# Nystrom attention and two gated MLPs on one core: landmark sums of the second batch by matrix products, softmax exponentials group by group, another order

## Chip, cores and metric

One core of a Trainium2 chip runs the kernel. The metric is the device time of one execution in microseconds (us), median over runs. The profile is of one further execution.

## What is computed

Everything is float32 in and out. The reference, cut to what matters:

```python
def _attn_ref(q, k, v):                       # q, k, v: 4 batches, 8 heads, 576 tokens, 64 wide
    q_lm = q.reshape(B, H, 32, 18, D).mean(axis=3)      # 32 landmarks, each the mean of 18 tokens
    k_lm = k.reshape(B, H, 32, 18, D).mean(axis=3)
    A, Bm, C = sm(q, k_lm), sm(q_lm, k_lm), sm(q_lm, k)   # scaled row softmax, with maximum and sum
    Z = Bm.transpose(0, 1, 3, 2) / (norm1(Bm) * norminf(Bm) + 1e-06)
    for _ in range(6):
        Z = 2 * Z - Z @ Bm @ Z
    return A @ Z @ C @ v
x = attn.transpose(0, 2, 1, 3).reshape(2304, 512)
x = ((x @ w_a) * (x @ w_b)) @ w_out             # 512 -> 1536 -> 512
h = x @ w_in; x = (h * tanh(softplus(h))) @ w_out2      # 512 -> 2048 -> 512
```

## The kernel before

The attention of batch b is a set of steps (function attention, from L132). kl and ql (lm_sum) sum groups of 18 tokens of k and q, which lie with (head, width) on the 128 partitions and the tokens along the row. sB and BB make the small softmax Bm, NS is one of six Newton steps for Z, sC0 and sC1 are the two halves of the scores of landmarks against all keys, whose maxima go to tile stC and whose exponentials to tile E; ET, U and M finish to a 128x128 matrix MT. A0 and A1 (function A) make the two halves of the scores of all queries against the landmarks, transpose them into tile sa (128 partitions x 576, that is 18 groups of 32 columns), subtract the maximum of each group and take the exponential; A0n and A1n (function An) divide by the sums of the groups, transpose back and store a high and a low part (tile at), since the matrix products of the MLPs run as three products of split float32 numbers.

MT is folded into the weights w_a and w_b (fold, named f0, f1, F0, F1 in the order, matrix products ps_bm<-wab,mt, result tile bm). The slots s0 to s11 are products of at and bm (ps_ab<-at,bm, 6 at a time) whose two halves are multiplied (tg, g); o0 to o7 are products with w_out (ps_o<-g,wo). Weights arrive as 64-bit words and are turned to float32 by the units c0 to c19 (to_f32, L366 to L384: one ScalarE and four VectorE instructions each; tiles stg, wab, f, wo). c0 to c3 make the first half of w_a and w_b that f0 needs, c4 to c7 the second, c8 to c11 the first w_out blocks.

Batches 0 and 1, the first twelve slots and c0 to c19 are recorded in the order of a written list (ORDER_1; + marks a step of batch 1, a digit a few filler products that nothing reads). VectorE, ScalarE and TensorE keep that order, so an instruction that waits holds all that stands behind it on its engine. GpSimd work and transfers are placed by the scheduler; every transfer is issued on SyncE's queue and they share 16 DMA engines. Behind ORDER_1 come the slots 12 to 95 with the steps of batches 2 and 3 between them (STEADY), then the second MLP, which the change does not touch.

By the subtraction for the fourth of the next w_out blocks, a little behind the end of ORDER_1 (wo<-f,wo, 136.79 us in the profile), both programs have done the same VectorE work apart from what the change adds and takes out; soon behind it their VectorE rows are the same, one by one.

Of the kernel before, what the change touches and what calls it, by code (L numbers as in the profile page):

```python
# [8 lines left out]
F32 = mybir.dt.float32  # L9
# [8 lines left out]
LM = 32  # L18
# [10 lines left out]


@with_exitstack
def nystrom_moe_kernel(ctx: ExitStack, tc: tile.TileContext, q, k, v, w_a, w_b, w_out1, w_in2, w_out2, out):
    nc = tc.nc
    NT = B * S
    gp = nc.gpsimd
# [41 lines left out]
    def bank(tag):  # L77
        return two.get(tag, ps).tile([128, 512], F32, tag=tag, bufs=2, name=f"ps_{tag}")
# [53 lines left out]
    def attention(ap, b, kt, qt, vt0=None):  # L132

        x = {}
        first = b == 0
# [2 lines left out]
        def sm(shape, nm, bufs=1, tag=None):  # L138
            return ap.tile(shape, F32, tag=tag or nm, bufs=bufs, name=nm)
# [3 lines left out]

        def lm_sum(src, nm):
            x[nm] = sm([128, 4, LM], nm)
            for j in range(0, 4, 2):
                if first and nm == "ql":
                    p = bank("o1")
                    for _ in range(3):
                        pe.matmul(p[:, 0:128], ident, x["kl"].rearrange("p j l -> p (j l)"), start=True, stop=True)  # L150
                held(ve.tensor_reduce(
                    out=x[nm][:, j:j + 2], in_=src[:, j:j + 2].rearrange("p j (t k) -> p j t k", k=BLK), axis=AX, op=ALU.add,
                ))
                yield
# [132 lines left out]
        def A(r):  # L287
            p = pair("A%d" % r)
            tile4(p, lambda o, rows, j: (o[:, 0:288], x["kl"][rows, j, :], qt[rows, j, 288 * r:288 * r + 288]))
            if r == 0:  # L290
                x["sa"] = sm([128, 2, 2, 288], "sa", tag="E")
            sa = x["sa"][:, r]
            yield
            for c in range(2):
                ve.transpose(out=sa[:, c], in_=p[:, c, 0:288])
            sa3 = sa.rearrange("p c (n l) -> p (c n) l", l=LM)
            ss = x["ss", r] = sm([128, 18, 4], "stA", 2)
            yield
# [41 lines left out]

    N_UNITS, N_SLOTS = 20, 12
    ORDER_1 = """
        kl kl ql ql c0 sB sC0 sB c0 sB sC1 4 c1 sB sC0 BB 2 c2 sC1 BB c3 sC1 NS 2 c1 sC1 c2 c3 sC1 c0 c1 NS
        ET0 NS c2 c3 NS 2 ET0 c0 ET1 NS NS c4 c1 A0 ET1 c2 NS 1 c5 A0 U NS c6 NS A0 NS c7 c3 NS A0 NS U NS c0
        NS NS c1 NS NS c2 M A0n M A1 c3 A0n f0 A0n f0 +kl A0n f0 A0n +kl | s0 +ql s0 s0 s1 +ql s1 A1 A1 +sC0
        +sC1 +sC0 A1 +sC1 A1n A1n A1n +sC1 A1n s0 c4 +sC1 A1n s1 c5 c6 +sC1 +sB s1 +sB s0 +ET0 c7 s1 s0 c4 +sB
        s2 +ET0 +sB s1 s2 +ET1 c5 c6 +BB +ET1 c7 c4 s2 c8 +BB +U s2 c5 s2 +NS +U s2 s3 +NS +NS c6 +NS s3 c7 s3
        +NS +NS c4 +NS c5 +NS +NS c6 +NS c7 +NS +NS f1 s3 c8 s3 c8 s3 +NS c8 f1 c8 +NS c9 +NS f1 +NS c8 +NS s4
        c9 +M c9 s4 s4 c9 +M c9 s5 s4 c9 +A0 c8 s5 c9 s4 s5 c10 s4 +A0 s6 s5 F0 c10 s6 c10 s5 +A0 c11 s5 s6 F0
        s7 s6 +A0 c11 +A1 c11 s7 s6 c11 s7 c12 s6 c11 +A0n c11 c11 +A0n +A0n F0 +A0n +A0n s7 F1 c10 s7 c10 s7  # L350
        F1 s8 c12 c12 c10 F1 s8 s8 c10 s9 s8 c12 o0 s9 s8 c12 s8 +A1 c13 s9 +A1 o0 s10 o1 s9 s10 c13 +A1 c13
        s9 c13 c14 s10 s9 c13 o1 s11 s10 c14 s10 o2 c14 s11 s10 c14 c15 c14 s11 o2 c15 c15 o3 +A1n c15 c16
        +A1n o4 o3 c16 c16 o5 c15 o4 c17 +A1n c17 +A1n o6 c17 o5 c16 +A1n c16 o7 o6 s11 c17 s11 s11 c17 c18 o7
        c18 c18 c18 c18 c19 c19 c19 c19 c19
    """

    def stage(src, shape, early):
# [626 lines left out]
```

## Time and profile before

| what | value |
|---|---|
| median of 3 runs | 856.5 us (854.84 to 857.36) |
| the profiled execution | 852.74 us, of which 850.7 us are the span of its instructions |
| TensorE busy | 794.7 us (93%), 5802 matrix instructions |
| VectorE busy | 565.8 us (67%) |
| ScalarE busy | 342.1 us (40%) |
| GpSimd busy | 153.2 us (18%) |
| DMA | 180.85 MB, mean 213 GB/s |

Times in the profile are microseconds from the span's start. A float32 product shows as two TensorE records. L56 is the line of the helper that records every ScalarE, VectorE and TensorE instruction; tiles tell them apart.

### The profile page before, as it was taken

Reading aid. Unit: us, or ns where it says so; the run is one execution under the profiler, and the core shown is the slowest. Engines: PE = TensorE matmul, PEld = TensorE weight load, DVE = VectorE, ACT = ScalarE, POOL = GpSimd, SP = SyncE. Lnnn points to the kernel's source line nnn. Section 1 sums busy time; section 2 is a strip of 40 time slices with the busy share of each in tenths; the row PEclk is TensorE's granted clock in tenths of the full one; section 3 lists DMA queues with packets and bytes.
Section 4 is the critical chain, followed back from the end, with each engine's and each line's share of the span. In section 5 each row is a group of like instructions: output and inputs, shape, how many; then the busy total and the mean of one; then the engine's idle time right before and its main releaser. Section 6 shows DMA issues by size and latency. Waiting matters only on the chain.

```text
span 850.7 us, 14559 instructions
## 1 busy us (share of the span) xinstructions
PE 794.7 (93%) x5802; PEld 691.9 (81%) x5802; DVE 565.8 (67%) x1027; ACT 342.1 (40%) x684; POOL 153.2 (18%) x144
## 2 busy tenths in 40 slices
PE   5666999999999999999988999999999999999997
PEld 4444887987887888787987898988988989988986
DVE  7899977895575488888985678768433347433433
ACT  3335454444323445444443444345332334332332
POOL 0011222222230232122234335320000000000000
PEclk9798899999999999999999899999999999999999
DMA  9736467458227338777376857788655445654501
GB/s 357 306 120 229 160 214 246 179 206 319 81 85 255 163 113 314 247 265 238 115 251 274 302 215 259 264 310 336 247 196 212 173 171 200 227 213 179 186 1 74
DMA packets 47891, 180.85 MB, mean 213 GB/s; under 512 B 4176, under 2 KB 12368, under 8 KB 38480
## 3 DMA queue, kind: packets, MB, share of 16 engines
q1 hardware_dynamic: 47824, 179.93, 58.9%
q8 instruction: 45, 0.74, 0.3%
q14 instruction: 22, 0.18, 0.1%
HBM read 126.44 MB, written 53.48 MB: 211 GB/s over the span
## 4 chain that ended last, share of the span: by engine, by line
PE 75%; DVE 14%; DMA 6%; issue 3%; ACT 2%; SPq 0%; POOL 0%; ACTq 0%; DVEq 0%
PE ps_ab L56 33%; PE ps_o L56 21%; PE ps_bm L56 11%; PE ps_at L56 10%; DVE f L56 5%; DMA kt<-in_k_dram 3%; DMA wi2d<-f 2%; DVE tg L56 1%; DVE f L378 1%; DVE bm L56 1%; DMA wo2d<-f 1%; DVE kl L56 1%; ACT f L374 1%; DVE x2acc L56 1%; DVE s L56 1%
## 5 line engine op out<-in xcount | busy, mean ns | idle before, releaser
L56 PE MATMUL ps_ab<-xc,wc 128*128 128x384 f32 x1008 | 201.7, 340 | 4.8 <-DVE u2s L56 3.1
L56 PE MATMUL ps_ab<-at,bm 128*128 128x288 f32 x1152 | 192.0, 307 | 13.4 <-DVE tg L56 6.9
L56 PEld LDWEIGHTS ps_ab<-at,bm 128*128 128x128 f32 x1152 | 165.4, 194 | 41.9 <-issue 11.8
L56 PEld LDWEIGHTS ps_ab<-xc,wc 128*128 128x128 f32 x1008 | 181.8, 189 | 16.9 <-DVE u2s L56 3.4
L56 PE MATMUL ps_o<-g,wo 128*128 128x288 f32 x1152 | 180.0, 298 | 3.1 <-DVE x2acc L56 2.1
L56 PEld LDWEIGHTS ps_o<-g,wo 128*128 128x128 f32 x1152 | 161.0, 188 | 15.4 <-issue 5.9
L519 POOL TENSOR_TENSOR g<-tg,g 128x288 fp32r<-128x288 f32 x96 | 87.1, 908 | 268.0 <-ACT g L56 268.0
L56 ACT ACTIVATE m<-c 128x384 f32<-128x384 f32 x96 | 50.2, 523 | 189.6 <-DVE c L56 189.5
L56 PE MATMUL ps_bm<-wo,g 128*128 128x512 f32 x288 | 95.5, 396 | 0.3 <-ACT g L56 0.3
L56 PE MATMUL ps_at<-wo,g 128*128 128x512 f32 x288 | 82.9, 395 | 0.0
L56 DVE TENSOR_TENSOR g<-m,g 128x384 fp32r<-128x384 f32 x96 | 66.7, 696 | 23.0 <-ACT g L56 23.0
L56 PE MATMUL ps_o<-wo,g 128*128 128x512 f32 x288 | 79.6, 393 | 0.0
L56 ACT ACTIVATE g<-tg 128x288 fp32r<-128x288 f32 x96 | 42.4, 442 | 79.9 <-DVE tg L56 79.7
L56 DVE SCALAR_TENSOR_TENSOR f<-stg,f 128x512 uint32<-128x512 uint32 x88 | 72.1, 823 | 1.6
L56 PEld LDWEIGHTS ps_at<-wo,g 128*128 128x128 f32 x288 | 54.3, 189 | 10.7
L56 DVE TENSOR_TENSOR tg<-ps_ab,ta 128x288 f32<-128x288 f32 x96 | 43.2, 451 | 29.7 <-PE ps_ab L56 21.9
L56 ACT ACTIVATE ta<-ps_ab 128x288 f32<-128x288 f32 x96 | 38.9, 405 | 57.4 <-PE ps_ab L56 56.9
L56 PEld LDWEIGHTS ps_o<-wo,g 128*128 128x128 f32 x288 | 53.6, 188 | 9.1
L56 PEld LDWEIGHTS ps_bm<-wo,g 128*128 128x128 f32 x288 | 53.7, 189 | 7.0 <-ACT g L56 0.6
L56 ACT ACTIVATE g<-m 128x384 fp32r<-128x384 f32 x96 | 50.3, 523 | 2.6
L56 DVE TENSOR_TENSOR c<-ps_ab,m 128x384 f32<-128x384 f32 x24 | 13.4, 557 | 50.6 <-PE ps_ab L56 50.6
L56 PE MATMUL ps_bm<-wab,mt 64*32 64x512 f32 x384 | 39.3, 644 | 6.2 <-DVE bm L56 6.2
(138 smaller groups left out, 755.1 us busy)
## 6 DMA issues: line engine op xcount, KB each, us to landing
wc<-wcd SPq DMA_DIRECT2D x16, 1792.0 KB, 7.3
wo<-wod SPq DMA_DIRECT2D x16, 1024.0 KB, 4.9
stg<-in_moe_w_out_dram SPq DMA_DIRECT2D x28, 512.0 KB, 4.5
wcd<-wc SPq DMA_DIRECT2D x8, 1792.0 KB, 7.1
wab<-wabd SPq DMA_DIRECT2D x10, 1024.0 KB, 6.3
stg<-in_moe_w_in_dram SPq DMA_DIRECT2D x16, 512.0 KB, 5.1
wod<-wo SPq DMA_DIRECT2D x8, 1024.0 KB, 6.7
stg<-in_moe_w_a_dram SPq DMA_DIRECT2D x12, 512.0 KB, 6.4
```

The lines of the kernel that those rows point to most:

```text
L56: i = f(*a, **kw)
L374: i = ac.engine.activation(dst, hi.bitcast(F32), AF.Abs)
L378: i = ve.engine.tensor_scalar(dst, dst, F32_TINY, F32_HUGE, op0=ALU.max, op1=ALU.min)
L519: gp.tensor_tensor(t[:, 1], tg, t[:, 0].bitcast(F32), op=ALU.subtract)
```

## The change

For batch 1 the landmark sums are no longer VectorE reductions over kt and qt. The host hands in two more inputs (q1, k1: tokens on 126 partitions, 7 groups of 18; five blocks of 512 columns), six transfers bring them in ahead of the second four weight blocks, and for each of 4 column blocks five products with a 126 x 7 matrix of ones (blk) write the sums to a PSUM bank; one ScalarE copy per tensor takes them out. In A, for batches 0 and 1, the subtraction and the single exponential over 576 columns are replaced by a small product (minus the scaled maximum) and 18 exponentials of 32 columns with the maximum as bias and the sum of the group as second output; An loses its sum. The low part of at goes to VectorE for all four halves of batches 0 and 1 (before: for the first alone, the others on GpSimd). ORDER_1 is another list; N_UNITS and N_SLOTS are the same.

```diff
+    blk = const.tile([128, 7], F32, name="blk")
+        ve.tensor_reduce(out=blk, in_=ident[:, 0:126].rearrange("p (l k) -> p l k", k=BLK), axis=AX, op=ALU.add)
+    def load_tokens():
+        out = []
+        for src in (k1, q1):
+            ts = []
+            for i in range(0, 5, 2):
+                if src is q1 and i:
+                    t = main.tile([128, 2, 2, S // 2], F32R, tag="AT", bufs=6, name="tok").bitcast(F32).rearrange("p a b s -> p (a b s)")
+                else:
+                    t = main.tile([128, 4, 288], F32, tag="x2", bufs=4, name="tok").rearrange("p a s -> p (a s)")
+                w = min(2, 5 - i)
+                nc.sync.dma_start(out=t[0:126, 0:DM * w], in_=src[:, DM * i:DM * (i + w)])
+                ts.append(t)
+            out.append(ts)
+        return out
...
         def lm_sum(src, nm):
             x[nm] = sm([128, 4, LM], nm)
+            if tokens:
+                p, ts = bank("o1"), tokens[nm == "ql"]
+                for j in range(4):
+                    for i in range(5):
+                        n, r = (4, 72) if i == 4 else (7, 126)
+                        f0 = DM * (i % 2) + 128 * j
+                        pe.matmul(p[:, LM * j + 7 * i:LM * j + 7 * i + n], ts[i // 2][0:r, f0:f0 + 128], blk[0:r, 0:n], start=True, stop=True)
+                    yield
+                ac.activation(x[nm].rearrange("p j l -> p (j l)"), p[:, 0:128], AF.Copy)
+                return
...
             ve.tensor_reduce(out=ss[:, :, 0], in_=sa3, axis=AX, op=ALU.max)
+            if b < 2:
+                ve.tensor_scalar(ss[:, :, 3], ss[:, :, 0], -SC_A, None, op0=ALU.mult)
+                for n in range(18):
+                    if n % 6 == 0:
+                        yield
+                    ac.activation(sa3[:, n], sa3[:, n], AF.Exp, bias=ss[:, n, 3:4], scale=SC_A, accum_out=ss[:, n, 1:2])
+                return
             ve.tensor_tensor(sa3, sa3, ss[:, :, 0:1].to_broadcast([128, 18, LM]), op=ALU.subtract)
...
-            ve.tensor_reduce(out=ss[:, :, 1], in_=sa3, axis=AX, op=ALU.add)
-            yield
+            if b > 1:
+                ve.tensor_reduce(out=ss[:, :, 1], in_=sa3, axis=AX, op=ALU.add)
+                yield
...
-            (ve if (b, r) == (0, 0) else gp).tensor_tensor(at[:, 1], af, at[:, 0].bitcast(F32), op=ALU.subtract)
+            (ve if b < 2 else gp).tensor_tensor(at[:, 1], af, at[:, 0].bitcast(F32), op=ALU.subtract)
...
-        kl kl ql ql c0 sB sC0 sB c0 sB sC1 4 c1 sB sC0 BB 2 c2 sC1 BB c3 sC1 NS 2 c1 sC1 c2 c3 sC1 c0 c1 NS
+        kl kl ql ql c0 sB sC0 sB c0 sB sC1 4 c1 sC0 sB c2 sC1 BB 2 sC1 c3 BB sC1 sC1 c2 NS 2 c1 c3 NS ET0 NS
...
     vt0 = load_v(ap, 0)
+    tokens = load_tokens()
     u0.prefetch(8)
     run0 = attention(ap, 0, kt, qt, vt0)
-    run1 = attention(ap, 1, *load_qk(ap, 1))
+    run1 = attention(ap, 1, *load_qk(ap, 1), None, tokens)
```

Three places of the new order. First VectorE, from the second half of An of batch 0's first half (af, at) to the maxima of batch 1's scores (stC). Before:

```order
L56 STREAM_TRANSPOSE af<-sa 128x288 x2
L56 TENSOR_REDUCE kl<-kt 128x64
L56 TENSOR_TENSOR bm<-ps_bm,bm 128x1024
L56 TENSOR_TENSOR at<-af,at 128x576
L56 TENSOR_REDUCE kl<-kt 128x64
L56 TENSOR_REDUCE ql<-qt 128x64 x2
L56 STREAM_TRANSPOSE sa<-ps_at 128x288 x2
L56 TENSOR_REDUCE stA<-sa 128x18
L56 TENSOR_TENSOR sa<-sa,stA 128x576
L56 TENSOR_REDUCE stC<-ps_at 128x2
L56 TENSOR_REDUCE stC<-ps_bm 128x2
```

With the change:

```order
L56 SCALAR_TENSOR_TENSOR wab<-stg,wab 128x2x256
L56 TENSOR_TENSOR at<-af,at 128x576
L413 TENSOR_SCALAR wab<-wab 128x2x256
L56 TENSOR_SCALAR wab<-wab 128x2x256
L56 STREAM_TRANSPOSE sa<-ps_at 128x288 x2
L56 TENSOR_TENSOR bm<-ps_bm,bm 128x1024
L56 TENSOR_REDUCE stA<-sa 128x18
L56 TENSOR_SCALAR stA<-stA 128x18
L56 SCALAR_TENSOR_TENSOR wab<-stg,wab 128x2x256 x2
L56 TENSOR_REDUCE stC<-ps_at 128x2
L56 TENSOR_REDUCE stC<-ps_bm 128x2
```

The four reductions kl and ql are gone, the conversions of c4 to c7 (wab) stand where they stood, and the subtraction (sa<-sa,stA) has become a product on stA alone.

Second TensorE, from the last Newton step of batch 0 (32x32) to the slot products behind batch 1's scores. Before:

```order
L56 MATMUL ps_at<-rz 32x32 x8
L56 MATMUL ps_at<-zd,U 64x128 x2
L56 MATMUL ps_at<-qt,kl 32x288 x8
L56 MATMUL ps_bm<-wab,mt 32x512 x8
L56 MATMUL ps_ab<-at,bm 128x288 x18
L56 MATMUL ps_at<-kt,ql 32x288 x8
L56 MATMUL ps_bm<-kt,ql 32x288 x8
L56 MATMUL ps_ab<-at,bm 128x288 x6
```

With the change, from the step M (zd,U) on:

```order
L56 MATMUL ps_at<-zd,U 64x128 x2
L56 MATMUL ps_o_443<-blk,tok 128x7 x4
L56 MATMUL ps_o_443<-blk,tok 128x4
L56 MATMUL ps_bm<-wab,mt 32x512 x8
L56 MATMUL ps_at<-qt,kl 32x288 x8
L56 MATMUL ps_o_443<-blk,tok 128x7 x4
L56 MATMUL ps_o_443<-blk,tok 128x4
L56 MATMUL ps_o_489<-blk,tok 128x7 x4
L56 MATMUL ps_o_489<-blk,tok 128x4
L56 MATMUL ps_ab<-at,bm 128x288 x6
L56 MATMUL ps_at<-kt,ql 32x288 x8
L56 MATMUL ps_bm<-kt,ql 32x288 x8
```

The products with the tokens (blk,tok; those of k write one bank, those of q the other) stand between the steps of batch 0, and batch 1's scores (kt,ql) come after 6 slot products and not after 18.

Third ScalarE, from the copies of ET of batch 0 to the copy of MT. Before:

```order
L56 ACTIVATE ET<-ps_p_331 128x512
L56 ACTIVATE ET<-ps_p_331 64x128
L374 ACTIVATE wab<-stg 128x2x256
L56 ACTIVATE rz<-ps_at 128x64
L374 ACTIVATE wab<-stg 128x2x256 x2
L56 ACTIVATE rz<-ps_at 128x64
L56 ACTIVATE sa<-sa 128x576
L56 ACTIVATE rz<-ps_at 128x64
L56 ACTIVATE mt<-ps_at 128x128
```

With the change:

```order
L56 ACTIVATE ET<-ps_p_342 128x512
L56 ACTIVATE ET<-ps_p_342 64x128
L56 ACTIVATE rz<-ps_at 128x64
L56 ACTIVATE sa,stA<-sa,stA 128x32 x6
L56 ACTIVATE rz<-ps_at 128x64
L56 ACTIVATE sa,stA<-sa,stA 128x32 x6
L56 ACTIVATE rz<-ps_at 128x64
L56 ACTIVATE sa,stA<-sa,stA 128x32 x6
L409 ACTIVATE wab<-stg 128x2x256 x3
L56 ACTIVATE mt<-ps_at 128x128
```

The 18 exponentials stand in three groups of six between the Newton steps' copies (rz), and the first instructions of c4, c5 and c6 have moved from ahead of them to behind them, ahead of the copy of MT.

## Rows read from the trace of the kernel before

**Rows 1.** Stretches: PE, PEld, DVE, ACT, POOL busy us (instructions), PEclk, DMA share, GB/s

```profile
10.00:30.00 20.00, 14.80 (x326) 9.98 (x327) 17.00 (x53) 10.11 (x24) 0.00 (x0) 0.87 1.03 405
0.00:44.27 44.27, 26.56 (x408) 18.59 (x408) 35.12 (x74) 14.50 (x30) 1.32 (x12) 0.85 0.83 321
24.50:41.45 16.95, 9.59 (x110) 6.28 (x103) 15.08 (x29) 3.59 (x9) 0.00 (x0) 0.71 0.77 304
44.27:86.80 42.53, 26.75 (x390) 18.10 (x390) 39.07 (x89) 18.57 (x42) 10.03 (x10) 0.87 0.51 184
86.80:137.48 50.68, 48.80 (x362) 43.01 (x355) 44.75 (x78) 27.18 (x57) 11.21 (x12) 0.97 0.65 209
137.48:850.70 713.22, 692.64 (x4652) 612.17 (x4650) 446.87 (x789) 281.82 (x555) 130.60 (x112) 0.99 0.58 208
```

**Rows 2.** Waits of TensorE, 44.27 to 137.48 us: total, times, longest

```profile
PE ps_bm L56 <- DVE bm L56: 5.7, 1, 5.7
PE ps_at L56 <- ACT E L56: 4.8, 1, 4.8
```

**Rows 3.** Waits of VectorE, the same stretch

```profile
DVE f L378 <- ACT f L374: 3.7, 1, 3.7
```

**Rows 4.** VectorE in order of time: start, us; idle before it at the end

```profile
33.66 1.35 DVE L56 TENSOR_REDUCE kl<-kt 128x64 f32<-128x1152 f32 x1 [1.56 <-DMA kt<-in_k_dram]
37.99 2.60 DVE L56 TENSOR_REDUCE ql<-qt 128x64 f32<-128x1152 f32 x2
43.52 0.75 DVE L56 TENSOR_REDUCE stC<-ps_bm 128x2 f32<-128x576 f32 x1
136.79 0.69 DVE L56 TENSOR_TENSOR wo<-f,wo 128x512 fp32r<-128x512 f32 x1 [0.33 <-ACT wo L56]
```

**Rows 5.** Groups of instructions by form, 0 to 140 us

```profile
L56 DVE TENSOR_REDUCE kl<-kt 128x64 f32<-128x1152 f32 x4 | 5.4, 1350 | 4.3 <-DMA kt<-in_k_dram 4.2
L56 DVE TENSOR_TENSOR sa<-sa,stA 128x576 f32<-128x576 f32 x8 | 6.4, 795 | 0.3
L56 DVE TENSOR_REDUCE stA<-sa 128x18 f32<-128x576 f32 x8 | 6.0, 749 | 0.1
L56 DVE TENSOR_SCALAR stA<-stA 128x18 f32<-128x18 f32 x4 | 0.7, 180 | 0.0
L56 DVE TENSOR_TENSOR at<-af,at 128x576 fp32r<-128x576 f32 x1 | 0.7, 748 | 0.0
L378 DVE TENSOR_SCALAR wab<-wab 128x512 f32<-128x512 f32 x17 | 8.0, 488 | 1.6 <-ACT wab L374 1.6
L56 DVE SCALAR_TENSOR_TENSOR wab<-stg,wab 128x512 uint32<-128x512 uint32 x32 | 23.6, 749 | 0.2
L56 ACT ACTIVATE sa<-sa 128x576 f32<-128x576 f32 x4 | 2.7, 682 | 1.3 <-DVE sa L56 1.2
L56 ACT ACTIVATE eb<-eb 128x64 f32<-128x64 f32 x2 | 0.5, 256 | 0.4 <-DVE eb L56 0.4
L56 ACT ACTIVATE E<-ps_bm,stC 128x288 f32<-128x288 f32 x4 | 1.8, 504 | 0.0
L56 ACT ACTIVATE ta<-ps_ab 128x288 f32<-128x288 f32 x19 | 7.7, 404 | 15.8 <-PE ps_ab L56 15.8
L56 ACT ACTIVATE rz<-ps_at 128x64 f32<-128x64 f32 x10 | 2.2, 222 | 4.5 <-PE ps_at L56 4.5
```

**Rows 6.** TensorE in order of time, 7 to 45 us

```profile
7.48 2.90 PE L56 MATMUL ps_o<-kl,ident 128*128 128x128 f32 x12 [7.48 <-DVE kl L56]
11.89 1.16 PE L56 MATMUL ps_o<-ident 128*128 128x128 f32 x8
41.45 0.91 PE L56 MATMUL ps_at<-kt,ql 64*32 64x288 f32 x16
42.16 0.69 PE L56 MATMUL ps_bm<-kt,ql 64*32 64x288 f32 x16
```

**Rows 7.** ScalarE in order of time, 43 to 50 us

```profile
47.73 0.87 ACT L56 ACTIVATE E<-ps_at,stC 128x288 f32<-128x288 f32 x2
```

More of the change, by code (lines that the diff above doesn't have):

```diff
@@ L31, in nystrom_moe_kernel @@
 @with_exitstack
-def nystrom_moe_kernel(ctx: ExitStack, tc: tile.TileContext, q, k, v, w_a, w_b, w_out1, w_in2, w_out2, out):
+def nystrom_moe_kernel(ctx: ExitStack, tc: tile.TileContext, q, k, v, w_a, w_b, w_out1, w_in2, w_out2, q1, k1, out):
     nc = tc.nc
@@ L130, in nystrom_moe_kernel, with attention @@
     PAIRS1 = {"ET0": "bm", "ET1": "bm"}
-    def attention(ap, b, kt, qt, vt0=None):
+    def attention(ap, b, kt, qt, vt0=None, tokens=None):
         x = {}
@@ L342, in nystrom_moe_kernel @@
     ORDER_1 = """
-        kl kl ql ql c0 sB sC0 sB c0 sB sC1 4 c1 sB sC0 BB 2 c2 sC1 BB c3 sC1 NS 2 c1 sC1 c2 c3 sC1 c0 c1 NS
[L344 to L352, printed above, removed]
@@ L353, in nystrom_moe_kernel @@
-        +A1n o4 o3 c16 c16 o5 c15 o4 c17 +A1n c17 +A1n o6 c17 o5 c16 +A1n c16 o7 o6 s11 c17 s11 s11 c17 c18 o7
-        c18 c18 c18 c18 c19 c19 c19 c19 c19
+        kl kl ql ql c0 sB sC0 sB c0 sB sC1 4 c1 sC0 sB c2 sC1 BB 2 sC1 c3 BB sC1 sC1 c2 NS 2 c1 c3 NS ET0 NS
+        c0 NS 2 c1 ET0 ET1 c3 c1 NS A0 ET1 NS c1 NS 1 A0 U NS A0 NS A0 c3 NS +kl U NS NS A0 c3 NS c0 +kl NS A0
+        c0 NS +ql c2 c2 NS A0n c4 +ql NS +ql c5 c2 A0n M c6 +kl c5 M c5 A0n c5 f0 c7 A0n A1 c7 f0 c7 +kl A1 c8
+        f0 +ql +kl A1 | s0 +ql c7 A1 +sC0 c5 +sC1 +sC0 s0 s0 A1 +sC1 s1 +sC1 A1 s0 c7 c6 s1 s1 A1n s0 s0 A1n
@@ new lines, in nystrom_moe_kernel @@
+        c6 +sC1 s1 c6 +sC1 +sB c6 A1n +ET0 +sB s1 A1n +sB s1 +ET0 +sB s2 +ET1 c4 s2 c4 +BB c4 +ET1 s2 c4 +BB
+        +U s2 c8 s2 +NS +U s2 s3 +NS +NS c8 +NS c8 s3 s3 +NS +NS c9 c8 +NS s3 f1 c8 c9 +NS +NS s3 c9 +NS c8 s3
+        f1 c9 +NS c10 +NS f1 +NS +NS +NS s4 c10 c9 +NS s4 c10 s4 c9 +NS s5 s4 c10 s4 +M s5 s4 c10 s5 +M c9 c10
+        s6 s5 c11 c10 +A0 s6 c11 s5 s6 c11 s5 c11 c12 s7 s6 c11 F0 s7 s6 +A0 c11 s6 s7 +A0 F0 +A1 c11 +A0 s7
+        o0 F0 +A0 c12 o1 c12 +A0 c12 c12 o0 c13 F1 +A0n o1 s7 o2 c13 F1 s7 +A0n F1 +A0n o3 o2 +A0n c13 s8 c13
@@ L355, in nystrom_moe_kernel @@
+        c14 c13 o3 o4 s8 c14 c14 c14 c15 s8 +A1 o4 s9 c15 s8 o5 s9 +A1 s8 s8 c14 +A1 s9 c15 c15 c16 s10 s9 +A1
+        c16 o6 c16 c16 s10 +A1 c15 s10 c16 o5 s11 +A1n o6 c17 o7 s9 s10 s11 +A1n s9 s10 c17 +A1n s11 s10 c17
+        o7 c17 +A1n c18 s11 c18 s11 c18 s11 c17 c19 c18 c19 c19 c18 c19 c19
     """
@@ L415, in step @@
                     self.prefetch()
-    wab = {}
+    wab, converted = {}, {}
     wabd = [dram.tile([128, 2048], F32, name=f"wabd{g}") for g in range(6)]
@@ L425, in conv @@
             yield from to_f32(t[:, 2 * jj:2 * jj + 2, i], st, True)
-            if (i, jj) == (1, 1):
+            converted[g] = converted.get(g, 0) + 1
+            if converted[g] == 4:
                 nc.sync.dma_start(out=wabd[g], in_=t.rearrange("p j i f -> p (j i f)"))
@@ L975 @@
         args.append(nc.dram_tensor(f"in_{name}_dram", a.shape, _mybir.dt.from_np(a.dtype), kind="ExternalInput").ap())
+    for name in "qk":
+        a = _np.pad(inputs[name].reshape(B, H, S, D)[1].transpose(1, 0, 2).reshape(S, DM), ((0, 54), (0, 0)))
+        a = arrays[f"in_{name}1_dram"] = _np.ascontiguousarray(a.reshape(5, 126, DM).transpose(1, 0, 2)).reshape(126, 5 * DM)
+        args.append(nc.dram_tensor(f"in_{name}1_dram", a.shape, _mybir.dt.from_np(a.dtype), kind="ExternalInput").ap())
     for i, (shape, dtype) in enumerate(_OUTS):
```

## The prediction

> **What bounds the kernel now.** The busy times by stretch come first [rows 1]. From 137.48 us to the end TensorE is busy for 692.6 of 713.2 us; the change moves nothing there, so what it wins or loses must be won or lost before, and then stays. From 86.80 to 137.48 us TensorE is busy for 48.8 of 50.7 us, VectorE for 44.8. From 44.27 to 86.80 us it is the other way round: VectorE has work for 39.1 of 42.5 us, TensorE for 26.8. The list of TensorE's waits then says what it stands still for: 5.7 us for VectorE's second part of a folded weight (bm), 4.8 us for ScalarE's exponentials of batch 1 (E) [rows 2]. Those in turn stood behind VectorE, whose order up to there holds four landmark reductions of batch 1, the first of which begins only when kt has landed, at 33.66 us, after 1.56 us of waiting [rows 4]. So the stretch up to 86.80 us is bound by VectorE, ahead of it by the transfers: from 10 to 30 us the DMA engines are full at 405 GB/s [rows 1].
>
> **What is taken from VectorE.** Four landmark reductions of 1.35 us (the ql pair took 2.60), 5.4 us; four subtractions of 0.795, 3.2 us; four sums of 0.749, 3.0 us [rows 4, 5]: 11.6 us. Added are four small products of 0.18 and three low parts of at of 0.748 that were GpSimd's, 3.0 us [rows 5], and one reduction for blk, about 0.4 us, by its size an estimate from the same rows, while VectorE waits for the first transfer. Net 8.2 us.
>
> **Where the lead arises.** I compare both programs at one point, the end of batch 1's second stC, 43.52 + 0.75 = 44.27 us before [rows 4], and from there to the end of the wo instruction at 136.79 + 0.69 = 137.48 us, by which both have done the same.
>
> First the point itself. The token copies are 2 x 126 x 2560 x 4 bytes = 2.58 MB, and they stand in the queue ahead of four weight blocks, a qt, three w_out blocks and batch 1's kt. At 405 GB/s they take 6.4 us, so kt lands at 33.6 + 6.4 = 40.0 us. Behind it TensorE needs 1.4 us for both scores (from 41.45 to 42.16 + 0.69 us) [rows 6] and VectorE one maximum more, 0.75 us: 42.1 us, **2.2 us earlier** than before, although kt is 6.4 us later, since four reductions no longer lie between. VectorE can be there: of its 35.1 us of work up to 44.27 us [rows 1] the reductions (5.4), two subtractions (1.6) and a sum (0.75) are gone, blk and two products (0.8) have come, and of c4 to c7, which came later before, the order now has four conversions of about 0.49 and three of 0.76 done, 4.2 us [rows 5]. That makes 32.3 us of work in 42.1 us.
>
> Then what is left. Behind the point VectorE had 93.2 us. Three of the sums and two of the subtractions lie there (3.8 us), two products and three low parts come in (2.6 us), and the 4.2 us of c4 to c7 are already done: **5.4 us less**.
>
> **What the 18 exponentials cost.** One replaces 0.68 us of ScalarE, 0.795 and 0.749 of VectorE, 2.2 us in a row. A ScalarE row of 576 columns takes 0.682 us, one of 64 takes 0.256 [rows 5]: 0.83 ns a column, so 32 columns take 0.23. A bias from a tile adds 0.10, by E (0.504) against ta (0.404), both 288 columns from PSUM [rows 5]. The second of two E rows ends 0.87 us after the first began, so successive ones overlap by about 0.12 [rows 7]: 0.21 us each, 3.9 us for 18. That is the low end, since no row here shows an exponential with a second output. The high end is a further small ScalarE operation behind each, 0.22 as for rz [rows 5], and no overlap: 0.55 us, 9.9 us for 18. I take 0.21, as E is the nearest row (same function, bias from a tile). A half of A is then later by 3.9 - 2.2 = 1.7 us. For batch 0 the wait for kt hides it (the slot products need only 6 before the scores); for batch 1 its products follow at once, and I charge **1.7 us** once.
>
> **What the token products cost.** 40 products are 80 records. Fillers of the same weights run at (1.16 - 0.33) / 7 = 0.12 us each, the cold ones behind the first kl at 2.90 / 12 = 0.24 [rows 6]: 9.5 to 19 us; for 7 columns instead of 128 it may be below that, and I take 0.16, 13 us. They go where TensorE waits: from 24.5 to 41.45 us it was busy for 9.6 of 17.0 us [rows 1], 7.4 us idle. Together 22.6 us must fit between 24.5 us and about 44 us, where the same 24 slot products and the scores are done; without stalls they do, at the low end with room for 7 us. The clock there was granted at 0.71 on average [rows 1]; denser work should raise it, and I count nothing for that. At the high end 6 us spill over, into the 15.8 us in which TensorE stood still from 44.27 to 86.80 us.
>
> **Costed at nothing:** the two ScalarE copies of the sums and the six issues on SyncE's queue, whose later issues wait for full DMA engines anyway; the late c4 to c7, whose instructions stand where VectorE has other work; MT's copy, now behind the first instructions of c4 to c6 and so behind transfers that land 6.4 us later: it comes about 1 us later than at 28.9 us, which the wait for kt hides. Without that cover each would delay the first slots by about its own length.
>
> **Sum.** -2.2 - 5.4 + 1.7 = **-5.9 us**. The profiled execution took 852.7 us, so 846.8; it lies 3.8 us below the median of the three runs, 856.5, which gives **850.6 us**. TensorE has room for it, since a gain of 5.9 us needs only a third of its 15.8 idle us.
>
> One rule speaks against it. All transfers in the trace of before have 128 partitions as their slowest dimension, and fill the engines (DMA share 1.03 from 10 to 30 us [rows 1]); none shows what 126 do. The Trainium skill (DMA: Bandwidth & Descriptors, "Why a DMA increments its semaphore by 16 and not by 1") has a transfer run on the largest number of engines up to 16 that divides that dimension, for 126 that is 14; by it kt would land an estimated 0.9 us later still and the sum be -5.0.
>
> **The rivals.**
>
> *The gaps close as well.* If the new order also fills TensorE's 5.7 us wait (o0 to o3 now stand before that fold) and VectorE's 3.7 us wait for a weight block [rows 2, 3], the gain is up to 5.9 + 5.7 = 11.6 us: 844.9. For it: the waits lie just where the order changes. Against: VectorE's 39.1 of 42.5 us leave it little.
>
> *No change: TensorE is paced by kt.* When the scores wait for kt until 40.0 us, the remaining 18 slot products come behind them. At 0.13 to 0.26 us each that is 43.8 to 46.1 us, against 43.8 before. If TensorE's own chain and not VectorE binds from there on, the lead is -2 to 0 us and the time 856.5 to 858.5. Against it: TensorE's largest two waits are for other engines.
>
> *Slower: the exponentials.* At 0.55 us each 72 of them put 39.6 us on ScalarE in place of 2.7. Batch 1's E stands behind 18 of them in ScalarE's order: from about 40 us on these last until 49.9, then two evictions of 0.8 us; E would begin at 50.7 instead of 47.73 us [rows 7], 3.0 us late. In each half of batch 1 18 stand ahead of evictions that free two PSUM banks, about 9.9 - 2 x 1.6 = 6.7 us, of which I let one part in two stay visible in each of the two halves, 6.7 in all. 3.0 + 6.7 less the 5.4 of VectorE's lead is +4.3: **860.8 us**. It decides from (47.7 - 40.8) / 18 = 0.38 us per exponential, where E is as late as before, and costs more than the lead from about 0.43. For it: nothing here shows the price of the second output. Against: the nearest row is well below.
>
> That the change does not do what it says I give no share: the VectorE order has no landmark reduction of batch 1 left.
>
> **How the numbers follow.** Forecast 0.50 (gain of 2.6 to 9 us), gaps closed 0.14, no change 0.20, slower 0.16. A difference under 0.3%, 2.6 us, cannot be told from none in this kernel. Faster is the first two, 0.64; within 0.3% 0.20; slower 0.16. The likeliest case's own range is 847.5 to 854. The range takes in the closed gaps down to 844.9 and, on the other side, no change with its 2 us, 858.5; most of the slower case is left out.
>
> **What would show it.** Right: no kl or ql reductions between 30 and 45 us, kt landing near 40 us, stC ending near 42, the wo instruction near 132, the waits behind it as before. An exponential of 32 columns at a pitch of 0.2 us shows the ScalarE term right; 0.4 or more, and E beginning after 48 us, would show it wrong. Token records at 0.16 us or less, and TensorE at the scores before 40 us, would show the token term right. The forecast falls if the stretch from 44 to 87 us is not shorter although VectorE has less to do in it, or if kt lands well after 41 us.

## The result, and the profile after

The changed kernel takes 844.47 us, median of four runs (844.01 to 850.3); the kernel before, beside it, 855.67. The ratio is 0.9883, 95% interval 0.9836 to 0.9929. The gain is 11.2 us, nearly twice the 5.9 forecast. My range, 844.9 to 858.5, was set from a kernel before at 856.5; set from the 855.67 beside it, it begins at 844.1, so the time lies at its low end. The profiled execution took 844.01 us, its span is 842.2 (before 852.74 and 850.7).

The sign was right. The place was not. Stretches of the profile after; columns as in [rows 1]:

```profile
10.00:30.00 20.00, 16.52 (x318) 12.46 (x316) 16.46 (x50) 12.39 (x54) 0.00 (x0) 0.93 1.03 298
30.00:50.00 20.00, 20.00 (x147) 15.58 (x147) 10.20 (x21) 9.42 (x36) 0.00 (x0) 0.50 0.96 384
0.00:44.27 44.27, 33.21 (x426) 26.48 (x426) 29.60 (x72) 18.94 (x64) 1.32 (x12) 0.81 0.98 333
44.27:86.80 42.53, 34.28 (x459) 25.88 (x459) 35.73 (x84) 25.56 (x95) 6.09 (x7) 0.88 0.62 225
86.80:137.48 50.68, 48.35 (x359) 40.21 (x358) 45.06 (x81) 35.65 (x115) 9.98 (x11) 1.00 0.67 219
137.48:842.20 704.72, 686.69 (x4645) 609.00 (x4643) 444.59 (x789) 280.73 (x553) 129.52 (x111) 0.99 0.59 210
```

VectorE has 110.4 us of work up to 137.48 us (29.60 + 35.73 + 45.06) where it had 118.9: 8.5 less, and I had put it at 8.2. But the time behind 137.48 us, in which I had expected nothing, is 8.5 us shorter, 704.72 against 713.22, and that is the whole difference of the spans. The two instructions between which I compared the programs, VectorE in order of time, to be held against [rows 4]:

```profile
49.66 0.76 DVE L56 TENSOR_REDUCE stC<-ps_bm 128x2 f32<-128x576 f32 x1 [0.20 <-PE ps_bm L56]
...
136.57 1.03 DVE L56 TENSOR_TENSOR wo<-f,wo 128x512 fp32r<-128x512 f32 x1
```

The end of the second stC comes at 50.4 us, 6.2 us later than before instead of 2.2 earlier; the wo instruction starts 0.2 us earlier and, being longer, ends 0.1 us later, instead of 5.9 earlier. The lead settles at 0.95 us by 145 us and is 8.0 us at the last output of the second MLP's hidden layer.

Why stC is late stands in TensorE's rows from 27 us on:

```profile
27.14 1.02 PE L56 MATMUL ps_o<-blk,tok 126*128 126x7 f32 x4 [0.68 <-DMA tok<-in_q_dram]
29.43 1.59 PE L56 MATMUL ps_o<-blk,tok 126*128 126x7 f32 x6 [1.27 <-DMA tok<-in_q_dram]
...
31.31 4.43 PE L56 MATMUL ps_o<-blk,tok 126*128 126x7 f32 x20
...
41.38 4.43 PE L56 MATMUL ps_o<-blk,tok 126*128 126x7 f32 x20
45.66 1.79 PE L56 MATMUL ps_ab<-at,bm 128*128 128x288 f32 x6
47.38 1.21 PE L56 MATMUL ps_at<-kt,ql 64*32 64x288 f32 x16
```

TensorE no longer waits from 30 to 50 us, but the clock granted there is 0.50, the 1.2 GHz level, all the time, although its records follow one another without a gap; before, it was 0.71 over the neighbouring stretch [rows 1]. A token record takes 0.22 us at that level (4.43 us for 20) and 0.13 ahead of it (1.28 for 10 at 25.18 us). The tokens themselves came late: from 10 to 30 us the DMA engines moved 298 GB/s, not 405, at the same share of 1.03. So batch 1's kt was issued at 31.7 us and landed 13.9 us later, at 45.6; I had 40.0.

The new operations, groups by form up to 140 us:

```profile
L56 ACT ACTIVATE sa<-sa,stA 128x32 f32<-128x32 f32 x72 | 22.0, 310 | 2.5 <-DVE stA L56 2.5
L56 ACT ACTIVATION_READ_ACCUMULATOR sa<-sa,stA 128x1 f32 x72 | 13.7, 190 | 0.0
L56 PE MATMUL ps_o<-blk,tok 126*128 126x7 f32 x64 | 13.5, 336 | 1.9 <-DMA tok<-in_q_dram 1.9
...
L56 PE MATMUL ps_o<-blk,tok 72*128 72x4 f32 x16 | 4.2, 331 | 0.3 <-DMA tok<-in_k_dram 0.3
```

An exponential with a sum is two instructions on ScalarE, the second a read of the accumulator; a pair comes every 0.305 us, 18 take 5.5 us. ScalarE around batch 1's E:

```profile
46.01 0.31 ACT L56 ACTIVATE sa<-sa,stA 128x32 f32<-128x32 f32 x1
...
51.48 0.31 ACT L56 ACTIVATE sa<-sa,stA 128x32 f32<-128x32 f32 x1
...
55.29 0.89 ACT L56 ACTIVATE E<-ps_at,stC 128x288 f32<-128x288 f32 x2 [2.54 <-DVE af L56]
```

E comes 7.6 us later than before [rows 7], behind the exponentials and behind af: sa and E share one buffer (both carry the tag "E" in attention), so E also waits for the transposes that read sa. TensorE waits 3.4 us for E (before 4.8 [rows 2]), and its 5.7 us for bm is gone:

```profile
PE ps_at L56 <- ACT E L56: 3.4, 1, 3.4
PE ps_at L56 <- DVE rz L56: 1.8, 1, 1.8
```

So the new order loses 7 us to 57 us and wins them back by 137. Where do the 8.5 us behind it come from? In this pair of profiles 0.95 us are there by 145 us, 3.3 come between 145 and 506 us, 3.8 in the second MLP and 0.5 behind the last output of its hidden layer. The 3.3 are no finding: the second profile of the changed kernel (a_again) loses 0.3 us in the same stretch against the same profile of before.

### The profile page after: what moved, and what is told of

Its sections match the earlier page's. It is cut to its first block, busy times and chain, and to the rows that moved or that the text cites. A ratio compares the mean times of both kernels' runs of the same rounds, so it can differ in the third digit from the quotient of the medians.

```text
span 842.2 us, 14866 instructions
## 1 busy us (share of the span) xinstructions
PE 802.5 (95%) x5882; PEld 701.6 (83%) x5882; DVE 555.0 (66%) x1023; ACT 360.9 (43%) x826; POOL 146.9 (17%) x141
## 4 chain that ended last, share of the span: by engine, by line
PE 73%; DVE 12%; DMA 7%; issue 3%; ACT 3%; POOL 0%; SPq 0%; DVEq 0%; ACTq 0%
PE ps_ab L56 32%; PE ps_o L56 20%; PE ps_bm L56 11%; PE ps_at L56 10%; DVE f L56 4%; DMA wi2d<-f 2%; DMA tok<-in_q_dram 2%; ACT sa L56 1%; DMA wo2d<-f 1%; DMA stg<-in_moe_w_a_dram 1%; DVE tg L56 1%; DVE f L413 1%; DVE wab L56 1%; ACT f L409 1%; DVE s L56 1%
## 5 line engine op out<-in xcount | busy, mean ns | idle before, releaser
L56 PE MATMUL ps_ab<-at,bm 128*128 128x288 f32 x1152 | 188.6, 304 | 6.0 <-DVE tg L56 4.8
L56 PEld LDWEIGHTS ps_ab<-at,bm 128*128 128x128 f32 x1152 | 162.2, 190 | 31.3 <-issue 8.6
L56 PEld LDWEIGHTS ps_o<-g,wo 128*128 128x128 f32 x1152 | 161.0, 189 | 20.4 <-issue 8.1
L56 DVE TENSOR_TENSOR g<-m,g 128x384 fp32r<-128x384 f32 x96 | 66.2, 690 | 23.5 <-ACT g L56 23.5
L56 DVE SCALAR_TENSOR_TENSOR f<-stg,f 128x512 uint32<-128x512 uint32 x88 | 69.9, 797 | 1.5
L56 DVE TENSOR_TENSOR c<-ps_ab,m 128x384 f32<-128x384 f32 x24 | 13.4, 557 | 48.2 <-PE ps_ab L56 48.2
L409 ACT ACTIVATE f<-stg 128x512 f32<-128x512 f32 x44 | 29.7, 675 | 31.7 <-DMA wi2d<-f 12.8
```

Source lines behind the costliest of these rows:

```text
L56: i = f(*a, **kw)
L409: i = ac.engine.activation(dst, hi.bitcast(F32), AF.Abs)
```

## The experiments

Medians in us; ratio to the runs of the kernel before on the same chip, with its 95% interval. These runs stand on four chips, on which the kernel before has 852.8 to 854.0, so a difference of two medians from the table is uncertain by 2 to 3 us. The last column is the time from the eleventh to the last output of the second MLP's hidden layer (g<-m) in the profile of each.

| label | what differs | median | ratio | g to g |
|---|---|---|---|---|
| (before) | | 852.8 to 854.0 | 1 | 330.73 |
| b_again | before, unaltered | 852.49 | 1.0002 (0.9986 to 1.0019) | 330.74 |
| b_pad32 | before, moved 32 bytes | 848.73 | 0.9948 (0.9926 to 0.9970) | 326.97 |
| b_pad64 | before, moved 64 bytes | 850.49 | 0.9971 (0.9953 to 0.9989) | 328.55 |
| a_again | changed, unaltered | 844.91 | 0.9899 (0.9876 to 0.9922) | 326.94 |
| a_shift64 | changed, moved 64 bytes | 845.73 | 0.9903 (0.9880 to 0.9926) | 328.51 |
| a_order | changed, sums and exponentials as before | 848.21 | 0.9935 (0.9912 to 0.9959) | 326.94 |
| a_dvesums | changed, sums on VectorE | 844.78 | 0.9894 (0.9871 to 0.9916) | 326.95 |
| a_oneexp | changed, one exponential per half | 850.19 | 0.9977 (0.9961 to 0.9993) | 326.95 |
| a_gplo | changed, low parts on GpSimd | 847.29 | 0.9928 (0.9905 to 0.9950) | 326.94 |
| a_together | changed, 18 exponentials in one piece | 853.04 | 0.9989 (0.9966 to 1.0012) | 326.93 |
| b_exps_pad32 | before, moved 32 bytes, exponentials per group | 863.60 | 1.0127 (1.0109 to 1.0144) | 326.97 |
| a_tok128 | changed, token transfers of 128 partitions | 840.77 | 0.9864 (0.9838 to 0.9891) | 326.93 |

### Where the tiles lie

blk is a tile of 28 bytes in the first pool of the left side of the on-chip memory (SBUF). It pushes every tile of the pools behind it (base, main, p1, p2) by 32 bytes. In the changed kernel TensorE runs the second MLP faster, with one wait of 0.3 us there in either kernel. Theory P is that the places of the tiles do it, theory R that the pace belongs to the execution or the chip. Three edits test it:

```diff
b_pad32 (b_pad64: 16 in place of 8)
+    pad = const.tile([128, 8], F32, name="pad")
+        gp.memset(pad, 0.0)
a_shift64
-    blk = const.tile([128, 7], F32, name="blk")
+    blk = const.tile([128, 16], F32, name="blk")
```

> The changed kernel once more, unaltered. In its profile the stretch up to the end of the wo instruction ends only 0.2 us earlier than in the profile of before, the lead is 0.95 us at 145 us, 2.0 at 250, 3.2 at 420, 4.0 at 490, and grows from there to 8.0 us at 840 us although TensorE is busy without a gap in both: successive products of 512 columns come every 0.2286 us instead of every 0.2315. Theory P (placement: blk's 28 bytes push every later tile of the left side of the memory by 32 bytes, and TensorE reads faster there): the pitch is 0.2286 us again and the time 844 to 845 us against 854 to 857 of before. Theory R (the pace belongs to the execution or to the chip, not to the kernel): the pitch comes out anywhere between 0.228 and 0.232, and the time between 844 and 850.

> The changed kernel with blk's tile 64 bytes wide instead of 28, of which 28 are used: every tile behind it moves by 64 bytes from its place in before instead of by 32. Same instructions, same order. Theory P: if the remainder of the address by 64 matters, the pitch in the second MLP is back at 0.2315 us and the time 4 us or so longer than the changed kernel's, 848 to 849 us. If what matters is only that it moved, no change. Theory R: the difference between this one and the changed kernel on the same chip is under 1 us.

> The kernel before with one more tile of 32 bytes, set once by GpSimd and read by nobody: every tile of the left side moves by 32 bytes as in the changed kernel, nothing else differs. Theory P: the pitch is 0.2286 us, and the time is 4 to 5 us below before, 851 to 852. Theory R: no difference from before within 1 us.

> The kernel before once more, unaltered: a second profile of it. In the five profiles since, successive products of the second MLP came every 173.5 to 173.8 ns (384 columns) and 228 to 229 ns (512 columns) in every kernel whose left side is moved by 32 bytes, 175.4 to 175.9 and 227 to 229 ns where it is moved by 64, and 175.4 to 175.7 and 230.4 to 231.9 ns in the one profile of before. Theory P (the places decide): 175.5 and 231 ns again, to half a nanosecond. Theory R (the execution decides): anything between, 173.5 and 228 as likely as not. The time is 851 to 858 us.

> The kernel before with a tile of 64 bytes set by GpSimd and read by nobody: the left side moves by 64 bytes. Theory P: as in the changed kernel at 64 bytes, 175.6 ns for 384 columns (the remainder by 64 is that of before) and 228 ns for 512: about half of the 4 us of the 32-byte shift, 850 to 852 us. If the extra GpSimd instruction and not the place made the kernel with 32 bytes faster, the pitches are those of before and the time is that kernel's, 848 to 849.

The two ends of the stretch on ScalarE (start, duration). The kernel before:

```profile
510.12 0.51 ACT L56 ACTIVATE g<-m 128x384 fp32r<-128x384 f32 x1
840.85 0.53 ACT L56 ACTIVATE g<-m 128x384 fp32r<-128x384 f32 x1
```

Its second profile (b_again):

```profile
507.76 0.51 ACT L56 ACTIVATE g<-m 128x384 fp32r<-128x384 f32 x1
838.50 0.53 ACT L56 ACTIVATE g<-m 128x384 fp32r<-128x384 f32 x1
```

The kernel before moved by 32 bytes:

```profile
511.55 0.51 ACT L56 ACTIVATE g<-m 128x384 fp32r<-128x384 f32 x1
838.52 0.52 ACT L56 ACTIVATE g<-m 128x384 fp32r<-128x384 f32 x1
```

Moved by 64 bytes:

```profile
510.58 0.51 ACT L56 ACTIVATE g<-m 128x384 fp32r<-128x384 f32 x1
839.13 0.53 ACT L56 ACTIVATE g<-m 128x384 fp32r<-128x384 f32 x1
```

The changed kernel:

```profile
505.89 0.51 ACT L56 ACTIVATE g<-m 128x384 fp32r<-128x384 f32 x1
832.84 0.52 ACT L56 ACTIVATE g<-m 128x384 fp32r<-128x384 f32 x1
```

330.7 us where nothing is moved, 328.5 at 64 bytes, 327.0 at 32, in 14 profiles to 0.05 us, whatever else the kernels do. Theory P holds and theory R falls: the places are worth 3.8 us in this stretch at 32 bytes and 2.2 at 64. The medians agree: 0.9948 of 854 is 4.4 us less, 0.9971 is 2.5. The successive starts of TensorE's records in the trace show which products: 384 columns come every 173.6 ns at 32 bytes and every 175.6 at 0 and 64; 512 columns every 227 to 229 ns at 32 and 64 and every 230 to 232 at 0. Which tile it is, and why, was not tried. Two expectations missed by size: a_shift64 was to lose 4 us if the remainder by 64 bytes matters, and loses 1.6 in the stretch and 0.8 by the median, since only the 384 columns return to the old pace; b_pad32 was put at 851 to 852 from a kernel before at 856, and the kernel before has 854.0 on that chip.

About 4 us of the gain are therefore no work of the change, and a pad in the kernel before has them too. The rest, by the medians 848.7 to 844.9 on one chip, is 3.8 us, with an uncertainty of 2 to 3.

### The parts of the change against each other

a_dvesums and a_oneexp take one part back, a_order both (for one exponential, ORDER_1 loses the last two entries of each half of A and gets one for its An):

```diff
a_dvesums, a_order
-    tokens = load_tokens()
-    run1 = attention(ap, 1, *load_qk(ap, 1), None, tokens)
+    run1 = attention(ap, 1, *load_qk(ap, 1))
-        ... +kl ... +kl ... +ql ... +ql ... +ql ... +kl ... +kl ... +ql +kl ... +ql ...
+        ... A1 +kl +kl +ql +ql +sC0 ...
a_oneexp, a_order
-            if b < 2:
-                ve.tensor_scalar(ss[:, :, 3], ss[:, :, 0], -SC_A, None, op0=ALU.mult)
...
-                return
-            if b > 1:
-                ve.tensor_reduce(out=ss[:, :, 1], in_=sa3, axis=AX, op=ALU.add)
-                yield
+            ve.tensor_reduce(out=ss[:, :, 1], in_=sa3, axis=AX, op=ALU.add)
+            yield
```

> The changed kernel with the landmark sums of batch 1 taken back to VectorE: no token transfers, no products with blk, four reductions of kt and qt behind the first maxima stA of batch 0's second half, just ahead of batch 1's scores; exponentials, low parts, blk's place and all else as in the changed kernel. It prices the token part alone. My forecast had the part at a gain (5.4 us of VectorE work taken off). By the trace it may have cost instead: stC ends at 50.4 us and not at 42.1, TensorE runs at the 1.2 GHz level from 30 to 50 us. If the token part is worth its 5.4 us the time is 849 to 850; if it only pays back what it costs, 844 to 846; if the late stC is its doing and nothing behind absorbs it, this one is faster, 840 to 842.

> The changed kernel with the exponentials of batches 0 and 1 taken back to one exponential per half with a subtraction and a sum on VectorE; token products, low parts, order and places as in the changed kernel (two entries of each half of A fewer, one of An more). To be compared with the changed kernel, 844.9 us. If the exponentials per group are what wins, it is 3 to 5 us slower, 848 to 850; if they win nothing, 844 to 846; if they cost, 841 to 843.

> The changed kernel without its token products and without its exponentials per group: landmark sums of batch 1 on VectorE just ahead of batch 1's scores, one exponential per half with subtraction and sum. What is left of the change is the new order, the low parts on VectorE and blk's 32 bytes. To be compared with the kernel before moved by 32 bytes, 848.7 us, and with the changed kernel, 844.9. If the order by itself is worth something: 845 to 847. If it is worth nothing without the parts that it was made for: 848 to 851; VectorE then has 8.2 us of work more than in the changed kernel. If the parts only pay together (either alone costs): 850 or more.

| landmark sums of batch 1 | one exponential per half | exponentials per group |
|---|---|---|
| VectorE | 848.2 | 844.8 |
| tokens on TensorE | 850.2 | 844.9 |

The order with the low parts shows no gain by itself (848.2 against 848.7). The exponentials per group win 3.4 to 5.3 us in it (3.5 to 6.7 by the ratios). The token products, the part on which my first term stood, win nothing: 0.1 us slower with the exponentials per group, 2.0 slower without (0.4 and 3.6 by the ratios).

The profiles show the same where all this work is done, at the 22nd output of the slots (g<-tg, ScalarE). In order: the kernel before, the changed kernel, a_order, a_oneexp, a_dvesums, and a_tok128, which is told below:

```profile
151.34 0.43 ACT L56 ACTIVATE g<-tg 128x288 fp32r<-128x288 f32 x1
150.40 0.43 ACT L56 ACTIVATE g<-tg 128x288 fp32r<-128x288 f32 x1
150.19 0.43 ACT L56 ACTIVATE g<-tg 128x288 fp32r<-128x288 f32 x1
152.82 0.43 ACT L56 ACTIVATE g<-tg 128x288 fp32r<-128x288 f32 x1
147.57 0.43 ACT L56 ACTIVATE g<-tg 128x288 fp32r<-128x288 f32 x1
147.60 0.43 ACT L56 ACTIVATE g<-tg 128x288 fp32r<-128x288 f32 x1
```

The tokens cost 2.6 to 2.8 us here with either form of the exponentials, and the groups win 2.4 to 2.6 with either form of the sums. Three profiles of the changed kernel's work (a_again and a_shift64 are the others) agree at this output to 0.5 us, but four with the old order, before, b_again, b_pad32 and b_pad64, lie between 149.4 and 154.2 us, so each of these numbers, from one profile a cell, is weaker than it looks. In the profile of a_dvesums stC ends 4.0 us earlier; why its median keeps nothing of the lead at this output, 3.8 us instead of 0.95, stays open. Behind it, up to 506 us, two profiles of the same program drift apart by 1.3 us (before and b_again) and by 3.6 (the changed kernel and a_again).

The low parts, by the medians, were a term with the wrong sign:

```diff
-            (ve if b < 2 else gp).tensor_tensor(at[:, 1], af, at[:, 0].bitcast(F32), op=ALU.subtract)
+            (ve if (b, r) == (0, 0) else gp).tensor_tensor(at[:, 1], af, at[:, 0].bitcast(F32), op=ALU.subtract)
```

> The changed kernel with the low parts of at of the three later halves of batches 0 and 1 back on GpSimd. It takes 2.2 us (three of 0.75) off VectorE and puts three on GpSimd, at about 2 us or more each by the rows of GpSimd's low parts of batches 2 and 3. If VectorE's work decides: 842 to 844. If the first slot products of a half wait for the low part: 845 to 848. My forecast had the part at a loss of 2.2 us.

847.3 against 844.9: on GpSimd they cost 2.4 us more, at the edge of what these medians can tell. One takes 1.53 us there and 0.75 on VectorE, and TensorE's weight loads wait 2.4 us in all for it. At the 22nd output of the slots only 0.4 us of this shows (150.79 against 150.40), so the price is not settled.

### Eighteen exponentials, and what stands behind them

b_exps_pad32 gives the kernel before the exponentials per group and keeps its order; a_together keeps the changed kernel's work and puts each half's exponentials in one piece:

```diff
b_exps_pad32 (ORDER_1: the fourth A0 and A1 of each batch three times, the first A0n and A1n of each gone)
+            if b < 2:
+                ve.tensor_scalar(ss[:, :, 3], ss[:, :, 0], -SC_A, None, op0=ALU.mult)
...
a_together (ORDER_1)
-        ... NS A0 NS A0 c3 NS +kl U NS NS A0 c3 NS c0 +kl NS A0
+        ... NS A0 NS A0 A0 A0 c3 NS +kl U NS NS c3 NS c0 +kl NS
```

> The kernel before, moved by 32 bytes, with the exponentials per group for batches 0 and 1 and nothing else of the change: its order as it was, except that each half of A has two entries more and each half of An one less. To be compared with the kernel before moved by 32 bytes, 848.7 us. It takes 5.5 us off VectorE (four subtractions and four sums go, four small products come), and puts 18 exponentials in place of one on ScalarE, which the trace of the changed kernel has at a pitch of 0.305 us, 5.5 us per half where the subtraction, exponential and sum took 2.2. If VectorE's work decides: 843 to 845 us. If the longer path of 3.3 us per half eats it: 848 to 849. If ScalarE binds, as my slower rival had it: 851 or more.

> The changed kernel with the 18 exponentials of each half of A in one piece where its order has them in groups of six with other work between (the fifth and sixth entry of a half moved right behind its fourth); same instructions, same work. The exponentials alone in the old order cost 15 us; there VectorE waited 4.2 us for the copy of a Newton step (rz) behind 18 exponentials. Theory I (what they stand ahead of on ScalarE decides): here two Newton steps' copies of batch 0 come behind 12 exponentials more, 3.7 us, and in the second halves evictions of slots do; the time is 848 to 852 against 844.9 of the changed kernel. Rival: the groups are of no account, since TensorE is busy without a gap from 30 to 50 us anyway and the loss in the old order lies elsewhere: 844 to 846.

In the old order they do not win 5 us but lose 15: 863.6 against 848.7, more than my slower rival gave. In the new order, put in one piece, they cost 8 us more than in groups of six (853.0, a little above the 848 to 852 expected), and 3 more than the single exponential (850.2; 1 by the ratios, which is within the noise). b_exps_pad32 shows how, first on ScalarE:

```profile
25.55 0.31 ACT L56 ACTIVATE sa<-sa,stA 128x32 f32<-128x32 f32 x1
25.77 0.19 ACT L56 ACTIVATION_READ_ACCUMULATOR sa<-sa,stA 128x1 f32 x1
...
31.04 0.20 ACT L56 ACTIVATE rz<-ps_at 128x64 f32<-128x64 f32 x1
```

and on VectorE:

```profile
31.27 0.22 DVE L56 TENSOR_TENSOR rz<-ps_at,rz 128x64 f32<-128x64 f32 x1 [4.16 <-ACT rz L56]
...
51.17 0.18 DVE L56 TENSOR_SCALAR stA<-stA 128x18 f32<-128x18 f32 x1 [3.78 <-ACT sa L56]
...
91.68 0.69 DVE L56 TENSOR_TENSOR wo<-f,wo 128x512 fp32r<-128x512 f32 x1 [4.67 <-ACT wo L56]
```

A copy of 0.2 us (rz) stands behind 5.5 us of exponentials, and VectorE, which keeps its order, stands with it; the third wait is of the same kind, for the copy of wo behind the 18 exponentials of batch 1. The second is another: there An needs the sums of the same exponentials and waits for their length. The three waits are 12.6 us. At the 22nd output of the slots the lag against the kernel before is 14.2 us (165.55 against 151.34), so most of the loss has arisen by then. a_together has the same wait at the first half, on VectorE:

```profile
27.60 0.23 DVE L56 TENSOR_TENSOR rz<-ps_at,rz 128x64 f32<-128x64 f32 x1 [4.45 <-ACT rz L56]
```

Theory I holds: with the same instructions the place in ScalarE's order makes 8 us, and the groups of six with other work between them are what makes this part pay.

### The token transfers

```diff
-                nc.sync.dma_start(out=t[0:126, 0:DM * w], in_=src[:, DM * i:DM * (i + w)])
+                nc.sync.dma_start(out=t[:, 0:DM * w], in_=src[:, DM * i:DM * (i + w)])
```

with two rows of zeros behind the 126 of each token input.

> The changed kernel with two rows of zeros behind the 126 token rows, so that each token transfer has 128 partitions; the products still read 126. In the trace of the changed kernel a packet of 4096 bytes of a token transfer took 267 ns, those of other transfers 161, and the DMA engines moved 240 GB/s over 12 us where they moved 405 before, at the same share of 1.04. Theory D (126 partitions make the transfers slow): the packets take 161 ns, the rate stays near 400 GB/s, kt and the weights of c4 to c7 land 4 to 4.5 us earlier, the end of batch 1's second stC comes 3 to 4 us earlier than 50.4 us, and the time falls by 0 to 3 us from 844.9, since what a_dvesums gained there it did not keep. Theory S (something else, as the place in HBM or in the queue, makes them slow): the packets and the time stay as they are.

A stretch of its profile, TensorE at batch 1's scores, and the issue of kt with its time to landing:

```profile
10.00:30.00 20.00, 17.90 (x341) 13.87 (x340) 16.66 (x52) 13.94 (x57) 0.00 (x0) 0.91 1.04 401
```

```profile
43.53 1.79 PE L56 MATMUL ps_ab<-at,bm 128*128 128x288 f32 x6
45.25 1.21 PE L56 MATMUL ps_at<-kt,ql 64*32 64x288 f32 x16
```

```profile
L111 SPq DMA_DIRECT2D kt<-in_k_dram x1: 328/328/328, 27.0 to 27.0; - x1
...
DMA to landing us min/median/max: 13.2/13.2/13.2
```

401 GB/s instead of 298; a packet of 4096 bytes takes 163 ns and not 267; kt lands at 40.2 us and not at 45.6 (44.4 to 46.1 in the six profiles with 126 partitions). Theory D holds.

The semaphore events in the traces add why: each token transfer of 126 partitions sent one event about 0.5 us after its issue and only 14 when data landed, each one of 128 partitions sent 16 and no early one; and of the four weight transfers behind the tokens two of 16 events come 4 to 9 us ahead of the others. So 14 of the 16 engines carried the tokens and two ran ahead, which is how the share could stay at 1.03.

The median is 840.77 us, 4 us below the changed kernel (3 by the ratios; of five runs one, 845.0, is no faster than it). stC ends at 48.2 us, 2.2 us earlier, where 3 to 4 were expected, and the lead at the 22nd output of the slots is that of a_dvesums, 3.7 us; why the medians of these two lie 4 us apart is open.

The scores still begin only at 45.25 us, behind the token products and six slot products, at a granted clock of 0.57 from 30 to 50 us: with the tokens in time TensorE's records have no gap from 23.5 to 50 us, and it is at the 1.2 GHz level from 26.6 to 47.0 all the same.

## Why the prediction was right or wrong, step by step

**Net work taken off VectorE, 8.2 us:** right, 8.5. That it becomes time: wrong for the most part. By the order, the sums, the low parts and the exponentials together 3.8 us were won, and none of it by the sums.

**The lead at stC, -2.2 us:** wrong, +6.2. Two steps failed. The first is "At 405 GB/s they take 6.4 us, so kt lands at 33.6 + 6.4 = 40.0 us". 126 partitions were what no transfer of before had, and I took the rate of 128. With 128 partitions kt does land at 40.2 us, so the sum was right for the shape that the change does not have; with 126 it lands 5.4 us later. The Trainium skill (DMA: Bandwidth & Descriptors, "Why a DMA increments its semaphore by 16 and not by 1") has such a transfer on 14 of 16 engines, by which I gave an estimated 0.9 us more. The trace agrees on the 14 engines, but they are a sixth of the price; the rest is that each packet takes 267 ns and not 163. Both together give 6.4 x 16/14 x 267/163 = 12.0 us, and the last landings of the transfers ahead and of the tokens lie 11.7 us apart (18.7 and 30.4 us). The same page of the Trainium skill ("The descriptor swizzle") has each engine write a port of its own in a transfer of 128 partitions; that other shapes share ports would fit the slower packets, but no run here shows it. The second is "Together 22.6 us must fit between 24.5 us and about 44 us": they did not, at the granted clock. That "denser work should raise it" is refuted for this work, since with the tokens in time TensorE's records had no gap and it was granted half. A token record took 0.22 us, not 0.16; the 80 took 17.7 us, not 13, near my high end of 19. This second step is the larger: of the 8.3 us by which stC is later than forecast (50.4 and 42.1), the padded transfers give back 2.2.

**5.4 us less VectorE work behind the point:** right in the work, 78.1 us from the end of stC to the end of the wo instruction against 83.8, 5.7 less. The time between the two fell by 6.0 us (87.2 against 93.2), where 5.4 - 1.7 = 3.7 was forecast, and just paid back the first term.

**The exponentials, 0.21 us each and 1.7 us once:** wrong in size, 0.305 with the accumulator read, between my ends; and wrong in kind. I charged a length, where what counts most is what stands behind them on ScalarE. The price by place runs from 3.4 to 5.3 us of gain to 15 us of loss. My slower rival had that mechanism, with a bound of 0.38 to 0.43 us per exponential for the new order; the old order lost 15 us at 0.305.

**Low parts on VectorE, 2.2 us of loss:** by the medians wrong sign, 2.4 us of gain; the trace shows 0.4 of it.

**"From 137.48 us to the end ... the change moves nothing there":** the step that failed most. The instructions are the same, their operands' places are not, and 4 of the gain's 9 to 11 us lie there. I had counted blk as one reduction of 0.4 us and not as a tile.

So the marks that I had set for "wrong" nearly all came (kt after 41 us, E after 48, TensorE's scores after 40, wo not near 132), and as far as the compared stretch goes the rival "TensorE is paced by kt" came nearest, with a lead of -2 to 0 us where -0.1 to 1 was measured. The time fell further than forecast for a reason that stood in none of the cases. That it lies in my range is luck: at the point where I looked for the whole gain, -5.9 us, the profiles show next to none, and the range reaches down to the measured time only by the closed gaps: TensorE's 5.7 us wait for bm did go, but it was among what paid back the late stC and is not the gain.

## What to carry to other kernels

A small tile in front of the pools moves everything behind it: before a gain is put down to the work, run the old kernel with a pad of the same size. An instruction split into many is priced by what stands behind it on its engine, so the split is worth only as much as the order that interleaves it. And the shape of a transfer that the profile has never shown is the first thing to bound: padding 126 partitions to 128 cost two rows of zeros and gave 3 to 4 us.

## What was not expected of the hardware

- Products of 512 and 384 columns with the granted clock at full run 1.2% apart (231.5 and 228.5 ns, 175.6 and 173.6) by where the tiles lie, by 32 or 64 bytes.
- Transfers of 126 partitions ran on 14 of 16 engines with packets of 267 ns instead of 163: the same share of the DMA engines, 1.03, and 298 GB/s instead of 401 to 405 over 20 us that were only partly theirs.
- TensorE was granted the 1.2 GHz level for 20.4 us (26.6 to 47.0) through records without a gap.
- A sum as second output of a ScalarE instruction adds an instruction of 0.19 us; for 32 columns the pair comes every 0.305 us.
- A moving operand of 7 columns made TensorE no faster: 0.13 us per record at 2.4 GHz and 0.22 at 1.2, as much as one of 128 columns (0.12 and 0.24 [rows 6]).
